# A fused attention and gated-MLP block on one core: first loads of x interleaved with the gate weights, the residual reloaded in four parts, and another hand-written order of the attention stage

## The chip, the cores and the metric

The kernel runs on one NeuronCore of a Trainium2 chip. The metric is the device time of one execution in microseconds (us). Before the change it is 266.06 us, the median of three runs (265.9 to 266.5).

## The reference

The inputs are x (2048 tokens by 512, bf16), the attention weights wqkv and wo, and the gate weights w_in, w_sp, b_sp and w_out. Cut to what matters:

```python
xn = layernorm(x)                                   # once, used by both branches
# A: attention, 32 heads of 16, a window of 256 tokens, causal
q, k, v = split(xn @ wqkv)
p = softmax(where(0 <= i - j < 256, q @ k.T / 4, -1e9))
A = (p @ v) @ wo
# B: gated MLP with mixing over tokens, F = 1376, Fh = 688
z = gelu_tanh(xn @ w_in)
z1, z2 = z[:, :Fh], layernorm(z[:, Fh:])
B = (z1 * (w_sp @ z2 + b_sp)) @ w_out
out = x + A + B
```

## The kernel before

The 2048 tokens are 16 blocks of 128. The program has no scheduler: every engine runs its instructions in the order in which the source writes them, and waits only on semaphores.

**First stage (L309 to L368).** x is loaded by SyncE (SP) in pairs of blocks (`load_x`, L189), the first pair as two single blocks. A block n goes through `stats` (L252: mean and variance on VectorE, DVE; the power -0.5 on GpSimd, POOL), `norm` (L258, DVE) and a transpose into `xnT`: blocks 0 to 5 by TensorE (PE) in `transpose_x` (L269), the others by a transposing DMA. `do_z(n, half)` (L279) multiplies block n with one half of w_in in 16 matmuls (4 chunks of the depth, columns 512 and 176), and ScalarE (ACT) applies the gelu. w_in comes in four DMAs (`load_win`, L203): two for the half z2, which `do_z(n, 1)` reads, and two for the half z1, which `do_z(n, 0)` reads. The last two, and the load of wqkv, are held back by a tiny DVE memset into the target (L313, L326). PE's order at the start is: 10 warm-up matmuls, transposes of block 0, 3 warm-up matmuls, transposes of block 1, `do_z(0, 1)`, `do_z(1, 1)`, transposes of block 2, `do_z(0, 0)`, transposes of block 3, and on.

**Attention stage (L568 to L601).** A list of tokens, `ORDER` (L49), is the order of the work. Each token issues a step:

- `qIIe`: the scores of tile II (four blocks of 128 keys by 128 queries, four head pairs), even or odd heads: PE matmuls that use a quarter of the array's rows each (L479), into two of the three double banks of the PSUM pool `ps_s`; then two exponentials on ACT (L487).
- `mII`: the masks of tile II, on POOL for a diagonal block (L498) and on DVE for the far edge of the window (L503).
- `aGw`, `AGw`: the values of head group G for a pair of query blocks w (L532, a quarter of the array's columns each), then on DVE a transpose and a reciprocal, and on POOL the division (`divide`, L546). `a` uses the single bank `ps_y`, `A` a double bank of `ps_s`; `C` and the `B` behind it share one double bank.
- `t`: DVE transposes a divided result into `oT` (L565).
- `pkGg`, `pqGg`, `pvGg` (`P`: into a bank of `ps_s`): a projection of k, q or v (L135, L151), emptied by DVE (L147, L161, L171).
- a number: so many matmuls of the token mixing w_sp @ z2 (L397). 32 of them make one block; at a block's first one, SP is given the transposing DMA of the next block of w_sp (L381). At the end of each half DVE forms z1 * (g + b) (L404), and SP transposes it for the output (`uT`, L420).
- `o`, `O`: one of the two parts of an output block: 4 matmuls with wo (L428), then 6 with w_out (L434), DVE's addition of the residual (L439), and the store (L440).

The residual: behind the last projection (L579 to L586) `xnT` is free, and SP loads x once more, into it, in four DMAs of 512 KB one after the other. The DMA for chunk c holds the blocks c, c + 4, c + 8 and c + 12.

SP's queue is in order, and holds all loads, the transposing DMAs and the stores but the last three. The matmuls of PE and their weight loads come to PE as a program of 6400 instructions, which is itself fetched by DMA while the kernel runs (queue q8 in the profile).

Of the kernel before, what the change touches and what calls it, by code (L numbers as in the profile page):

```python
# [8 lines left out]
P = 128  # L9
BF = mybir.dt.bfloat16  # L10
# [5 lines left out]
D = 512  # L16
# [5 lines left out]
NB = S_TOK // P  # L22
NDC = D // P
# [23 lines left out]


ORDER = """  # L49
pv11 Pk03 q000 1 pq03 2 q001 2 pq10 1 q010 9 m00 q011 1 pk10 q020 3 m01 2 a00 1 q021 10 q030  # L50
pk11 4 m02 q031 10 q040 2 pv03 q041 4 m03 t 1 pk12 q050 6 m04 1 q051 1 a01 3 q060 pk13 3 m05
q061 4 a02 1 q070 8 q071 a03 1 t 3 q080 pv10 2 m07 2 q081 pq11 3 m06 1 q090 pq12 4 q091 a04 3
m08 q100 2 pk20 2 q101 9 q110 pv12 1 t 1 m10 3 q111 1 pv13 1 m09 q120 5 pq21 q121 3 t 1 a05 m11
q130 2 m12 8 q131 pq20 4 q140 t t 2 pk21 q141 3 A06 a07 A10 q150 4 m13 7 q151 2 pq13 q160 m14 6
a11 q161 3 t 6 q170 1 t pv20 1 t q171 3 m16 5 m15 3 q180 4 pq23 q181 1 m17 8 q190 t a12 6 q191 1
pk23 3 m18 3 q200 6 m19 4 q201 a13 C14 B15 q210 t 2 pv21 4 q211 5 m20 3 q220 2 pk22 Pv23 3 m21
q221 3 pq31 q230 10 q231 pq30 2 m23 q240 4 pq22 2 m22 q241 7 t 1 q250 a16 1 t 3 q251 1 m24 2 t 3
Pv30 6 q260 pk32 3 t q261 2 A20 a17 A21 q270 11 q271 m26 pk30 4 q280 t 10 q281 2 pv31 4 q290 1
m25 2 m28 7 q291 2 pv22 q300 1 m27 9 q301 m29 6 A22 m30 a23 q310 8 q311 3 t 5 pk33 q320 1 m31
Pq33 3 a24 q321 2 t 7 t q330 3 pq32 t Pk31 q331 pv33 4 q340 2 m32 3 m33 3 q341 4 pv32 m34 1 q350  # L60
2 t 10 q351 3 a30 A25 t A26 a27 q360 10 q361 3 t o 1 q370 1 m35 1 o m36 q371 3 m37 5 t q380 3 o
1 q381 4 o q390 A31 a32 1 t 2 t 1 t q391 8 m39 q400 3 o 1 q401 o 1 O q410 2 O 1 o 3 m38 q411 1 o
q420 1 m40 5 A33 a34 q421 O t 2 O 1 q430 2 t m42 m41 o 1 q431 2 o q440 m43 4 O 2 O 1 A35 a36
q441 3 O m44 O o o t 5 A37 1 t O O t 2 o o 1 O O 6 O 1 O O O O O
"""


# [1 line left out]
def kernel(  # L69
# [12 lines left out]
    nc = tc.nc  # L82
    x2 = A_x.flatten_outer_dims()
# [5 lines left out]
    xnT = pers.tile([P, NDC, S_TOK], BF, name="xnT")  # L89
# [27 lines left out]
    def rpow(dst, var, n):  # L117
        v = sml.tile([P, NB], F32, name="rs_v")
        nc.vector.tensor_scalar(out=v[:, :n], in0=var, scalar1=LN_EPS, scalar2=None, op0=ALU.add)  # L119
        nc.gpsimd.tensor_tensor(out=dst, in0=v[:, :n], in1=negh[:, :n], op=ALU.pow)  # L120
# [3 lines left out]
    def bank(name, ring):  # L124
        if ring:
            return ps_s.tile([P, 2, 512], F32, name=name, tag="S")[:, 0, :]
        return ps_y.tile([P, 512], F32, name=name, tag="y")[:]
# [50 lines left out]
    with tc.tile_pool(name="win_pool", bufs=1) as winp, tc.tile_pool(  # L178
        name="xsp", bufs=8
# [6 lines left out]
        make_identity(nc, ident[:])  # L186
        xs_tiles = {}

        def load_x(n2, split=False):  # L189
            xs = xsp.tile([P, 2, D], BF, name="xs")  # L190
            if split:
                for j in range(2):
                    r = (2 * n2 + j) * P
                    nc.sync.dma_start(out=xs[:, j, :], in_=x2[r : r + P, :])  # L194
            else:
                nc.sync.dma_start(
                    out=xs[:],
                    in_=x2[2 * n2 * P : (2 * n2 + 2) * P, :].rearrange("(j p) d -> p j d", p=P),
                )
            for j in range(2):  # L200
                xs_tiles[2 * n2 + j] = xs[:, j, :]

        def load_win(half, c0, c1):  # L203
            nc.sync.dma_start(  # L204
                out=w_in_sb[:, c0:c1, half * FH : (half + 1) * FH],
                in_=B_w_in[c0 * P : c1 * P, half * FH : (half + 1) * FH].rearrange(
                    "(c p) f -> p c f", p=P
                ),
            )

        load_x(0, split=True)
        load_win(1, 0, 2)
        load_win(1, 2, 4)
        load_x(1)
        warm = sml.tile([P, 1], F32, name="warm")
        nc.scalar.activation(out=warm[:], in_=esel[:, 0:1], func=ACT.Gelu_apprx_tanh)

        nc.gpsimd.affine_select(
            out=fmask[:], in_=fmask[:], pattern=[[-1, P]], compare_op=ALU.is_gt,
# [3 lines left out]
            out=esel[:], in_=esel[:], pattern=[[-32, 4]], compare_op=ALU.is_ge,  # L223
# [3 lines left out]
            out=esel[:], in_=esel[:], pattern=[[32, 4]], compare_op=ALU.is_ge,  # L227
# [24 lines left out]
        def stats(n):  # L252
            st = sml.tile([P, nc.vector.BN_STATS_DIM], F32, name="st")
            nc.vector.bn_stats(out=st[:], in_=xs_tiles[n])  # L254
            nc.vector.bn_aggr(out=mvx[:, n, :], in_=st[:])
            rpow(rstdx[:, n : n + 1], mvx[:, n, 1:2], 1)

        def norm(n):  # L258
            xn = xnp.tile([P, D], BF, name="xn")
            nc.vector.tensor_scalar(  # L260
                out=xn[:], in0=xs_tiles[n], scalar1=mvx[:, n, 0:1],
                scalar2=rstdx[:, n : n + 1], op0=ALU.subtract, op1=ALU.mult,
            )
            if n >= X_DMA:
                nc.sync.dma_start_transpose(out=xnT[:, :, n * P : (n + 1) * P], in_=xn[:])
            else:
                xn_tiles[n] = xn
# [11 lines left out]
        def do_z(n, half):  # L279
            zp2 = ps_s.tile([P, 2, 512], F32, name="zs", tag="S")  # L280
            zp = zp2[:].rearrange("p a q -> p (a q)")
            f0 = half * FH
            for c in range(NDC):
                for lo, hi in Z_RANGES:
                    nc.tensor.matmul(  # L285
                        zp[:, lo:hi],
                        lhsT=xnT[:, c, n * P : (n + 1) * P],
                        rhs=w_in_sb[:, c, f0 + lo : f0 + hi],
                        start=(c == 0),
                        stop=(c == NDC - 1),  # L290
                    )
            dst = z1_all if half == 0 else z2_all
            nc.scalar.activation(out=dst[:, n, 0:FH], in_=zp[:, 0:FH], func=ACT.Gelu_apprx_tanh)  # L293
# [28 lines left out]
        transpose_x(1)  # L322
        do_z(0, 1)
        stats(2)
        stats(3)
        nc.vector.memset(wqkv[0:1, 0, 0:1], 0.0)  # L326
        load_x(3)
        nc.sync.dma_start(out=wqkv[:], in_=A_wqkv.rearrange("(c p) f -> p c f", p=P))
        for n2 in range(4, NB // 2):
            load_x(n2)  # L330
        norm(2)
        do_z(1, 1)
        transpose_x(2)
        stats(4)
# [3 lines left out]
            out=emask[:, 0:1], in_=esel[:], op=ALU.add, axis=mybir.AxisListType.X  # L338
        )
        nc.vector.tensor_scalar(  # L340
            out=emask[:, 1:2], in0=emask[:, 0:1], scalar1=-1.0, scalar2=1.0,
# [74 lines left out]
    def load_uT():  # L416
        n = len(uT_tiles)
        if n < NB and n < NB - (len(g_steps) + 2 * NB - 1) // (2 * NB) and n <= max(out_n[0], 0) + 3 - (out_n[0] < 0):
            uT = utp.tile([P, NFC, P], BF, name="uT")
            nc.sync.dma_start_transpose(out=uT[:], in_=z1_all[:, n, :])  # L420
            uT_tiles[n] = uT
            load_uT()

    def out_part(n, fo, c0, c1, part):
# [16 lines left out]
            out=out2[n * P : (n + 1) * P, c0:c1], in_=xr  # L441
        )

    def output(ring):
        n, part = o_steps.pop(0)
        last = n == NB - 1
        if part == 0:
            out_n[0] = n
            load_uT()
            fo_tiles[n] = bank("fo", ring)  # L450
        out_part(n, fo_tiles[n], 0, D - LAST * last, part)
        if last and part == 1:
            fo = bank("fo", not ring)
            for part in range(2):
                out_part(n, fo, D - LAST, D, part)
# [106 lines left out]
    def finish():  # L562
# [9 lines left out]
        out=w_out_sb[:, 0:5, :], in_=B_w_out[0:640, :].rearrange("(c p) n -> p c n", p=P)  # L572
# [1 line left out]
    nc.sync.dma_start(out=w_out_sb[0 : FH - 5 * P, 5, :], in_=B_w_out[5 * P : FH, :])  # L574
    tokens = ORDER.split()
    last_proj = max(i for i, t in enumerate(tokens) if t[0] in "pP")
    xres = {}
    for i, t in enumerate(tokens):
        if i == last_proj + 1:  # L579
            for n in range(NB):  # L580
                xres[n] = xnT[:, n % NDC, (n // NDC) * D : (n // NDC + 1) * D]
            for c in range(NDC):
                nc.sync.dma_start(
                    out=xnT[:, c, :].rearrange("p (m d) -> p m d", d=D),
                    in_=x2.rearrange("(m c p) d -> c p m d", p=P, c=NDC)[c],
                )  # L586
        if t[0] == "q":
            scores(int(t[1:3]), int(t[3]))
        elif t[0] == "m":
            masks(int(t[1:3]))  # L590
        elif t[0] in "aABC":
            values(int(t[1]), int(t[2]), t[0])
        elif t[0] == "t":
            finish()
        elif t[0] in "pP":
            proj(t[1], int(t[2]), int(t[3]), ring=t[0] == "P")
        elif t[0] in "oO":
            output(t[0] == "O")
        else:
            for _ in range(int(t)):  # L600
                mix()  # L601
# [30 lines left out]
```

## Time and profile before

| what | value |
|---|---|
| median of 3 runs | 266.06 us |
| the profiled execution: its time | 267.51 us |
| the profiled execution: its span, first to last instruction | 265.8 us |
| PE busy | 256.3 us, 96% |
| ACT, DVE, POOL busy | 205.6, 197.7, 122.0 us |
| granted clock of PE | 1.000 |
| mixing matmuls (L397) | 512, busy 95.1 us |
| exponentials (L487) | 180, busy 168.9 us |
| x again, as the residual | 4 DMAs of 512 KB, 5.6 us each to landing |

The page of the profile gives one execution: busy time by engine, the span in slices, the DMA queues, the chain of work that ended last, and the costliest groups of instructions. Matmuls overlap one another, so a busy PE is not one at its peak. The profiled execution took 1.45 us longer than the median, and 1.71 us of its time lie outside the span.

### The profile page before, as it was taken

The numbers are of one execution on the slowest core, as the hardware profiler recorded it, in microseconds if no ns is written. First come the engines' busy times: TensorE is split into PE (matmuls) and PEld (weight loads), VectorE is DVE, ScalarE is ACT, GpSimd is POOL, SyncE is SP. The second block draws the span as 40 slices with busy tenths as digits, with TensorE's granted clock in tenths as the row PEclk, the third lists the DMA queues.
The fourth block names the chain that finished last, engine by engine and source line by source line (L and its number), as shares of the span: only waits on it lengthen the run. The fifth ranks groups of instructions, "written<-read, shape, count | busy, mean of one in ns | idle before, by whom it ended". The sixth has DMA issues, their size and how long they took to land.

```text
span 265.8 us, 7432 instructions
## 1 busy us (share of the span) xinstructions
PE 256.3 (96%) x3166; PEld 143.1 (54%) x3199; DVE 197.7 (74%) x384; ACT 205.6 (77%) x233; POOL 122.0 (46%) x140
## 2 busy tenths in 40 slices
PE   7799999999999999999999999999998999999995
PEld 3465665654545555555575456655574454545543
DVE  4799999667687788788797778897868473686532
ACT  3577767689999999999988989988887986782000
POOL 4243445215442663758454556455468344365100
PEclk9999999999999999999999999999999999999999
DMA  6693122950405072230330323651369263434433
GB/s 212 217 337 62 39 42 59 169 180 2 109 2 112 0 111 22 62 81 2 79 81 2 79 44 41 72 52 40 81 194 226 60 131 77 73 82 71 118 78 83
DMA packets 61216, 23.83 MB, mean 90 GB/s; under 512 B 52304, under 2 KB 60672, under 8 KB 61184
## 3 DMA queue, kind: packets, MB, share of 16 engines
q1 hardware_dynamic: 60704, 23.06, 40.2%
q8 instruction: 25, 0.41, 0.7%
q10 hardware_dynamic: 432, 0.30, 0.4%
q0 software_dynamic: 48, 0.00, 0.3%
q14 instruction: 7, 0.06, 0.1%
HBM read 8.41 MB, written 2.10 MB: 40 GB/s over the span
## 4 chain that ended last, share of the span: by engine, by line
PE 93%; DMA 2%; DVE 1%; issue 1%; SPq 1%; DVEq 0%
PE gf L397 31%; PE zs L285 13%; PE S L479 12%; PE m L151 10%; PE o_t L532 8%; PE fo L434 8%; PE m L135 6%; PE fo L428 5%; DMA xs<-in_A_x_dram 2%; DVE st L254 0%; PE tp L274 0%; SPq L204 0%; DVE xnT L439 0%; SPq L194 0%; DVE o_c L548 0%
## 5 line engine op out<-in xcount | busy, mean ns | idle before, releaser
L487 ACT ACTIVATE E<-S 128x1024 bf16<-128x1024 f32 x180 | 168.9, 1043 | 17.9 <-PE S L479 9.1
L397 PE MATMUL gf<-z_all,wspT 128*128 128x344 bf16 x512 | 95.1, 311 | 1.0 <-issue 1.0
L498 POOL TENSOR_SCALAR_AFFINE_SELECT E<-E 128x1024 bf16<-128x1024 bf16 x64 | 79.2, 1259 | 32.4 <-ACT E L487 32.2
L397 PEld LDWEIGHTS <-wspT 128*128 128x128 bf16 x512 | 44.1, 98 | 36.9 <-issue 16.5
L503 DVE TENSOR_TENSOR E<-E,fmask 128x1024 bf16<-128x1024 bf16 x56 | 52.6, 967 | 2.6 <-ACT E L487 2.5
L554 POOL TENSOR_TENSOR o_norm<-o_c,rsum 128x256 bf16<-128x256 f32 x32 | 21.5, 671 | 62.0 <-DVE rsum L552 59.3
L285 PE MATMUL zs<-w_in_sb,xnT 128*128 128x512 bf16 (+1 forms) x249 | 39.1, 307 | 0.4
L479 PE MATMUL S<-q_ring,k 32*128 32x128 bf16 (+2 forms) x760 | 37.2, 267 | 0.0
L293 ACT ACTIVATE z_all<-zs 128x688 bf16<-128x688 f32 x32 | 23.8, 744 | 12.8 <-PE zs L285 12.8
L151 PE MATMUL m<-xnT,wqkv 128*128 128x512 bf16 x111 | 31.5, 380 | 1.0 <-issue 0.2
L285 PEld LDWEIGHTS <-xnT 128*128 128x128 bf16 x256 | 22.2, 98 | 14.9
L404 DVE SCALAR_TENSOR_TENSOR z_all<-gf,b_all,z_all 128x344 bf16<-128x344 f32 x32 | 18.2, 567 | 15.3 <-PE gf L397 15.3
L548 DVE STREAM_TRANSPOSE o_c<-o_t 128x512 f32<-128x512 f32 x32 | 22.3, 697 | 7.2 <-PE o_t L532 6.5
L479 PEld LDWEIGHTS <-k 32*128 32x128 bf16 x760 | 12.7, 92 | 25.9 <-issue 25.2
L439 DVE TENSOR_TENSOR xnT<-fo,xnT 128x512 bf16<-128x512 f32 (+2 forms) x17 | 11.2, 659 | 17.2 <-PE fo L434 17.2
L532 PE MATMUL o_t<-E,v 128*32 128x128 bf16 (+1 forms) x1080 | 23.4, 238 | 0.0
L434 PE MATMUL fo<-w_out_sb,uT 128*128 128x512 bf16 (+2 forms) x101 | 23.3, 366 | 0.1
L532 PEld LDWEIGHTS <-v 128*32 128x32 bf16 x1080 | 19.2, 97 | 5.1 <-issue 4.6
L120 POOL TENSOR_TENSOR rstdx<-rs_v,negh 128x1 f32<-128x1 f32 x16 | 10.3, 646 | 18.3 <-DVE rs_v L119 16.9
L171 DVE TENSOR_TENSOR k<-m,emask 128x1024 bf16<-128x1024 f32 x13 | 15.8, 1218 | 3.2 <-PE m L151 3.0
L151 PEld LDWEIGHTS <-wqkv 128*128 128x128 bf16 x128 | 11.7, 98 | 11.6 <-issue 1.7
L135 PE MATMUL m<-wqkv,xnT 128*128 128x128 bf16 x256 | 16.9, 219 | 0.2 <-DVE o_c L548 0.2
(51 smaller groups left out, 173.2 us busy)
## 6 DMA issues: line engine op xcount, KB each, us to landing
xnT<-in_A_x_dram SPq DMA_DIRECT2D x4, 512.0 KB, 5.6
xs<-in_A_x_dram SPq DMA_DIRECT2D x7, 256.0 KB, 6.7
out_dram<-xnT SPq DMA_DIRECT2D x13, 128.0 KB, 1.7
wqkv<-in_A_wqkv_dram SPq DMA_DIRECT2D x1, 1536.0 KB, 6.3
w_in_sb<-in_B_w_in_dram SPq DMA_DIRECT2D x4, 344.0 KB, 4.8
w_out_sb<-in_B_w_out_dram SPq DMA_DIRECT2D x1, 640.0 KB, 6.2
wo_sb<-in_A_wo_dram SPq DMA_DIRECT2D x1, 512.0 KB, 5.1
xs<-in_A_x_dram SPq DMA_DIRECT2D x2, 128.0 KB, 2.0
```

Of the source, the lines that this page charges most:

```text
L135: nc.tensor.matmul(m[:, j * P : (j + 1) * P], lhsT=xnT[:, c, n * P : (n + 1) * P], rhs=wqkv[:, c, 2 * D + G * P : 2 * D + (G + 1) * P], st ...
L151: nc.tensor.matmul(m, lhsT=wqkv[:, c, w0 : w0 + P], rhs=xnT[:, c, grp * 512 : (grp + 1) * 512], start=(c == 0), stop=(c == NDC - 1),)
L285: nc.tensor.matmul(zp[:, lo:hi], lhsT=xnT[:, c, n * P : (n + 1) * P], rhs=w_in_sb[:, c, f0 + lo : f0 + hi], start=(c == 0), stop=(c == NDC ...
L293: nc.scalar.activation(out=dst[:, n, 0:FH], in_=zp[:, 0:FH], func=ACT.Gelu_apprx_tanh)
L397: nc.tensor.matmul(gf[:, 0:FQ], lhsT=wsp_tiles[n][:, c, :], rhs=z2_all[:, c, lo : lo + FQ], start=(c == 0), stop=(c == NB - 1),)
L434: nc.tensor.matmul(fo[:, c0:c1], lhsT=uT_tiles[n][:, c, :], rhs=w_out_sb[:, c, c0:c1], start=False, stop=(c == NFC - 1),)
L479: nc.tensor.matmul(S[:, h2, j * P : (j + w) * P], lhsT=k_t[(G, kb // 4)][32 * s : 32 * s + 32, e, (kb % 4) * P : (kb % 4 + 1) * P], rhs=q_ ...
L487: nc.scalar.activation(out=E[:, j : j + 3 : 2, 0:nb, :].rearrange("p h b c -> p h (b c)"), in_=tiles[pr][:, :, 0 : nb * P], func=ACT.Exp, ...
L498: nc.gpsimd.affine_select(out=E[:, :, j, :], in_=E[:, :, j, :], pattern=[[0, 8], [1, P]], compare_op=ALU.is_ge, fill=0.0, base=0, channel_ ...
L503: nc.vector.tensor_tensor(out=E[:, :, j, :], in0=E[:, :, j, :], in1=fmask[:].unsqueeze(1).to_broadcast([P, 8, P]), op=ALU.mult,)
L532: nc.tensor.matmul(T[32 * s : 32 * s + 32, e, j * P : (j + l) * P], lhsT=v_t[(G, kb // 4)][:, kb % 4, s, e : e + 2, :].rearrange("p a d -> ...
L548: nc.vector.transpose(out=C[:, 0 : 32 * DH], in_=Tb)
```

## The change

There are three edits.

1. *The first loads.* `load_x` loses its split form. A new `load_block` loads one block. The order on SP was block 0, block 1, two DMAs for the z2 half of w_in, the pair of blocks 2 and 3; it is now block 0, block 1, first z2 DMA, block 2, second z2 DMA, block 3. And on DVE `norm(2)` now stands right behind `stats(2)`; it stood behind `stats(3)` and behind the memset that releases wqkv.
2. *The residual.* A new `load_xres(c)` loads the blocks 4c to 4c + 3 into chunk c of `xnT`. Part 0 is loaded behind the last projection; the parts 1, 2 and 3 when the output of the blocks 0, 4 and 8 begins, so each is asked for four blocks ahead.
3. *`ORDER`* is another list. It has the same steps: 90 score tokens, 45 mask tokens, 39 projections, 32 values, 32 `t`, 32 output parts and 512 mixing matmuls. It has 146 runs of mixing matmuls where there were 155, and two `C`/`B` pairs where there was one.

```diff
-        def load_x(n2, split=False):
+        def load_block(n):
+            if n % 2 == 0:
+                xs_pairs[n // 2] = xsp.tile([P, 2, D], BF, name="xs")
+            xs_tiles[n] = xs_pairs[n // 2][:, n % 2, :]
+            nc.sync.dma_start(out=xs_tiles[n], in_=x2[n * P : (n + 1) * P, :])
+
+        def load_x(n2):
             xs = xsp.tile([P, 2, D], BF, name="xs")
...
-        load_x(0, split=True)
+        load_block(0)
+        load_block(1)
         load_win(1, 0, 2)
+        load_block(2)
         load_win(1, 2, 4)
-        load_x(1)
+        load_block(3)
...
         stats(2)
+        norm(2)
         stats(3)
         nc.vector.memset(wqkv[0:1, 0, 0:1], 0.0)
...
-        norm(2)
         do_z(1, 1)
...
+    def load_xres(c):
+        part = xnT[:, c, :].rearrange("p (m d) -> p m d", d=D)
+        for m in range(4):
+            xres[4 * c + m] = part[:, m, :]
+        nc.sync.dma_start(
+            out=part, in_=x2[4 * c * P : (4 * c + 4) * P, :].rearrange("(m p) d -> p m d", p=P)
+        )
...
         if part == 0:
             out_n[0] = n
+            if n % 4 == 0 and n + 4 < NB:
+                load_xres(n // 4 + 1)
             load_uT()
...
         if i == last_proj + 1:
-            for n in range(NB):
-                xres[n] = xnT[:, n % NDC, (n // NDC) * D : (n // NDC + 1) * D]
-            for c in range(NDC):
-                nc.sync.dma_start(
-                    out=xnT[:, c, :].rearrange("p (m d) -> p m d", d=D),
-                    in_=x2.rearrange("(m c p) d -> c p m d", p=P, c=NDC)[c],
-                )
+            load_xres(0)
```

Of the order, two places that the prediction speaks of (before above, after below):

```diff
-a01 3 q060 pk13 3 m05 q061 4 a02
+a01 3 q060 1 m05 1 pk13 2 q061 9 q070 a02
...
-m33 3 q341 4 pv32 m34 1 q350 2 t 10 q351 3 a30 A25 t A26 a27 q360 10 q361 3 t o
+m32 pv32 1 q340 5 t 4 q341 pv30 4 m33 3 q350 m34 9 A30 A25 a26 q351 5 t 1 t 2 q360 8 o
```

More of the change, by code (lines that the diff above doesn't have):

```diff
@@ L49 @@
 ORDER = """
[L50 to L61, printed above, removed]
@@ L62 @@
-1 q381 4 o q390 A31 a32 1 t 2 t 1 t q391 8 m39 q400 3 o 1 q401 o 1 O q410 2 O 1 o 3 m38 q411 1 o
-q420 1 m40 5 A33 a34 q421 O t 2 O 1 q430 2 t m42 m41 o 1 q431 2 o q440 m43 4 O 2 O 1 A35 a36
-q441 3 O m44 O o o t 5 A37 1 t O O t 2 o o 1 O O 6 O 1 O O O O O
+Pq10 Pk03 q000 pq03 3 q001 3 pv11 q010 5 m00 5 q011 pk10 1 m01 1 q020 10 q021 4 pk11 m02 q030 8
+q031 2 a00 5 q040 1 pv03 2 q041 t 2 m03 1 pk12 q050 10 m04 q051 1 a01 3 q060 1 m05 1 pk13 2 q061
+9 q070 a02 4 q071 a03 2 t 2 q080 t pv10 m06 4 q081 pq12 4 q090 m07 pq20 2 A04 q091 pq11 1 m08
@@ new lines @@
+q100 4 pk20 q101 9 q110 pv12 2 m10 2 q111 pv13 4 q120 m09 pq21 3 q121 1 m11 4 a05 q130 t 1 m12 3
+t a06 q131 9 q140 2 t 1 Pq22 a10 A07 q141 m13 1 pk21 1 t 1 q150 9 q151 4 pq13 q160 3 t m14 6
+q161 a11 4 q170 3 pv20 1 m16 q171 2 t m15 1 pq23 1 q180 7 t 2 q181 2 pv21 m17 1 q190 m18 15 q191
+C12 B13 a14 m19 q200 9 q201 3 pv23 1 q210 3 pk23 q211 10 t q220 6 pk22 q221 1 m20 9 q230 6 pq31
+q231 2 t m21 2 a15 q240 1 t 5 m22 4 q241 2 pq30 m23 2 q250 2 t 7 q251 5 a20 C16 B17 q260 11 q261
+1 m24 pv31 4 m26 q270 pk32 4 q271 6 t 4 q280 2 pk31 q281 3 m25 1 t 2 Pk33 5 q290 5 t a21 q291 2
@@ new lines @@
+m27 7 q300 a22 2 m28 5 q301 Pq32 pv22 Pk30 q310 11 q311 4 m29 1 a23 A24 q320 pq33 1 t 3 q321 9
+m31 1 q330 1 m30 1 pv33 t q331 6 m32 pv32 1 q340 5 t 4 q341 pv30 4 m33 3 q350 m34 9 A30 A25 a26
+q351 5 t 1 t 2 q360 8 o m35 q361 t 2 t 4 m36 2 q370 3 o 1 q371 4 m37 o q380 o 3 q381 A31 a32 A27
+t q390 8 q391 2 m38 3 o q400 o q401 1 m39 7 t O 1 t q410 2 O m40 o 3 q411 2 o 2 q420 A33 a34 4 t
+t 2 q421 m42 1 o 1 q430 1 o O 1 q431 O 1 o m41 q440 1 m43 o O 2 O A35 a36 t t q441 O O 2 O O o
+m44 o 2 A37 O 3 t 5 O 4 o o O O O O
@@ L187 @@
         xs_tiles = {}
-        def load_x(n2, split=False):
-            xs = xsp.tile([P, 2, D], BF, name="xs")
[L191 to L195, printed above, removed]
-                nc.sync.dma_start(
-                    out=xs[:],
-                    in_=x2[2 * n2 * P : (2 * n2 + 2) * P, :].rearrange("(j p) d -> p j d", p=P),
-                )
+        xs_pairs = {}
+        def load_block(n):
[4 more added lines that the diff above has]
+        def load_x(n2):
+            xs = xsp.tile([P, 2, D], BF, name="xs")
+            nc.sync.dma_start(
+                out=xs[:],
+                in_=x2[2 * n2 * P : (2 * n2 + 2) * P, :].rearrange("(j p) d -> p j d", p=P),
+            )
             for j in range(2):
@@ L442, in out_part @@
         )
+    xres = {}
+    def load_xres(c):
+        part = xnT[:, c, :].rearrange("p (m d) -> p m d", d=D)
+        for m in range(4):
+            xres[4 * c + m] = part[:, m, :]
+        nc.sync.dma_start(
+            out=part, in_=x2[4 * c * P : (4 * c + 4) * P, :].rearrange("(m p) d -> p m d", p=P)
+        )
     def output(ring):
@@ L576 @@
     last_proj = max(i for i, t in enumerate(tokens) if t[0] in "pP")
-    xres = {}
     for i, t in enumerate(tokens):
         if i == last_proj + 1:
-            for n in range(NB):
-                xres[n] = xnT[:, n % NDC, (n // NDC) * D : (n // NDC + 1) * D]
-            for c in range(NDC):
-                nc.sync.dma_start(
-                    out=xnT[:, c, :].rearrange("p (m d) -> p m d", d=D),
-                    in_=x2.rearrange("(m c p) d -> c p m d", p=P, c=NDC)[c],
-                )
+            load_xres(0)
         if t[0] == "q":
```

## The prediction

> **What bounds the kernel now.** I read the page first: the busy times, then the shares of the chain that ended last.
>
> ```profile
> PE 256.3 (96%) x3166; PEld 143.1 (54%) x3199; DVE 197.7 (74%) x384; ACT 205.6 (77%) x233; POOL 122.0 (46%) x140
> ...
> PE 93%; DMA 2%; DVE 1%; issue 1%; SPq 1%; DVEq 0%
> ```
>
> PE is the bound, in both stages. So only two things can move the time: holes in PE's work, and PE work that becomes longer or shorter. ACT, DVE and POOL matter where they make PE wait. Next I went through PE's rows in order of time and looked for steps longer than the same step elsewhere. There are two large holes. The first is near the start. In the chain in order of time:
>
> ```profile
> 2.71 5.55 DMA xs<-in_A_x_dram
> 8.28 0.70 DVE st L254
> 9.38 0.61 DVE st L254
> 10.39 0.35 DVE xn L260
> 10.78 0.40 PE tp L274 x4
> 11.18 1.17 PE zs L285 x8
> ```
>
> Blocks 2 and 3 land at 8.26. DVE then makes the statistics of both before it norms block 2. PE had finished `do_z(1, 1)`, and its transposes of block 2 begin at 10.78. The timeline gives the hole ahead of them:
>
> ```profile
> 10.78 0.40 PE L274 MATMUL tp<-ident,xn 128*128 128x128 bf16 x4 [1.79 <-DVE xn L260]
> ```
>
> The second hole is at 202, two score tokens after the residual loads. From PE's and SP's timelines there:
>
> ```profile
> 201.63 0.41 PE L479 MATMUL S<-q_ring,k 32*128 32x384 bf16 x8
> 203.02 0.61 PE L397 MATMUL gf<-z_all,wspT 128*128 128x344 bf16 x3 [0.98 <-issue]
> ...
> 194.08 2.03 SPq L583 DMA_DIRECT2D xnT<-in_A_x_dram  x4
> 197.40 6.16 SPq L381 DMA_TRANSPOSE wspT<-in_B_w_sp_dram  x1
> ```
>
> The same pair of steps takes 0.34 elsewhere and 1.39 here: 1.05 us lost, in which PE waited for nothing that the profile shows. The DMA rows of two windows, 188 to 200.5 and 200.5 to 206, give the reason that I take:
>
> ```profile
> q14 instruction: 1, 0.01, 0.2%
> ...
> q8 instruction: 2, 0.03, 2.4%
> ```
>
> q8 moves PE's program, 25 transfers in all (page). 0.41 MB for a program of 6400 instructions is one transfer per 256. In the 12.5 us before 200.5 there is none, though PE issued some 480 instructions in them; then come two in 5.5 us. Meanwhile the four residual loads keep the DMA engines full (204 GB/s and a DMA share of 0.95 over 194 to 208). I read the hole as PE out of instructions, because the fetch came late. Besides these two, the attention stage loses some 0.9 us in pieces of at most 0.3.
>
> **First loads.** Blocks 0 and 1, and the first z2 DMA, keep their places; that DMA lands at 5.0 (1.73 issue, 3.3 to landing). The next 344 KB landed 0.98 us later (2.19 + 3.8), so 128 KB cost about 0.36: block 2 lands near 5.4, the second z2 DMA near 6.35 instead of 6.0. `do_z(0, 1)` starts at 6.50 and needs that DMA for its fifth to eighth pair of matmuls, from about 7.1: covered by 0.7. DVE is free at 6.2. Block 2 takes 0.69 statistics, 0.18, 0.15, POOL's 0.55, 0.41 norm, with gaps 2.2 in all (the rows from 8.28 on), so it is normed at 8.4, and PE, done near 8.9, finds it ready. `norm(2)` now waits some 0.7 for POOL with `stats(3)` behind it on DVE; block 3 isn't there before 8.26, so this costs nothing as long as it lands then. SP has one more issue (0.45) ahead of the loads of the z1 half; those waited for DVE's memset until 4.04 anyway.
>
> The hole closes, but what is late next? `do_z(0, 0)` would start at 9.1 and needs the z1 half. Its two DMAs have the same bytes ahead of them as before, and the slowest load of w_in took 6.4 from its issue at 4.45: 10.84. Then half of that step is left, 1.17/2 = 0.58, so block 3's transposes come at 11.48 instead of 12.18: **-0.7**, not -1.9. Block 3 is normed by then (8.45 plus two statistics and a norm: 10.96). From there to 56 us PE has no hole in the trace and everything hangs on PE's own pace, so the 0.7 is carried. Bounds: 15 of the 16 parts of each of these loads landed about 1.5 us earlier than the last, so one DMA engine was late. Without it in a run, block 3's norm sets the transposes: 12.18 - 11.04 = -1.1 against this trace. But a run without it had little hole before either: blocks 2 and 3 at 6.7, transposes of block 3 at 10.75, and DVE's wait for POOL now makes that 11.04: **+0.3**. I take -0.7, the value of the rows.
>
> **Residual in four parts.** Part 0 alone stands ahead of the next w_sp transpose, 512 KB instead of 2 MB. A transposing DMA's issue took 6.16 behind four loads and 1.45 to 1.95 without; behind one I estimate 3. PE's fetch waits behind a quarter as much. The parts 1 to 3 go into SP's queue ahead of a uT transpose and a store; the uT is used three blocks later, and each part four blocks later, over 10 us against 5.6 to landing. Part 0 is asked for some 8 us of PE work before the first output part: covered; without that cover DVE's addition, and with it the bank, would wait. So the hole goes: **-1.05**. Bounds: 0 (the loads are not its cause) and -1.05.
>
> The Trainium skill, page "DMA: Bandwidth & Descriptors", section "Queues, rings and completion order", speaks against this: each DMA engine takes turns between its queues, a packet at a time. By that rule a fetch on its own queue would not stand behind 2 MB of another, the hole would stay, and the sum would be -1.0. The trace leans the other way (no q8 transfer for 12.5 us, then two in 5.5).
>
> **The order.** The same matmuls are issued, so I count the joints. A mixing run takes 0.143 a matmul. Followed by a projection, its last one takes 0.16; followed by scores or values, 0.25. So each step from the whole array into its row or column parts costs 0.1. There are 93 in the old list, 91 in the new: -0.2. Nine fewer runs of mixing and the other neighbours (medians of each token by what follows it) make up to -0.46. I take **-0.3**.
>
> New waits? The bank `ps_y` first. From the end of one user to the start of the next, less DVE's row for emptying it (v and q 0.69, k 1.22, values 0.69 to 0.72), the old list has 0.04 too little once (`pk10` to `a00`), and 0.19 once; the smallest in the new is 0.33 (outputs aside). Values: `A30` comes 4.1 after `q341`, where `a30` came 5.1 after. The mask takes 0.44 + 2 x 0.92 for the exponentials and 1.09 to 1.55 on POOL: 3.4 to 3.9. Just enough; bound +0.3. The two `C`/`B` pairs hold a double bank for some 3 us; behind each stand 9 or 11 mixing matmuls before the second score token: 0. ACT needs 1.81 per score token and gets one every 1.8 to 2.0 in the first 60 us in both lists: 0. The tail ends with four output parts and the same last store: 0.
>
> Sum: -0.70 - 1.05 - 0.30 = -2.05. The profiled 267.51 would become 265.5; the median, 1.45 lower, 266.06 - 2.05 = **264.0**.
>
> **The rivals.**
>
> - *The start gives nothing* (the late DMA engine belongs to the profiled run): for it, the 1.45 that this run lies above the median is just the engine's lateness. 266.06 + 0.3 - 1.35 = 265.0; at +0 264.7.
> - *The second hole stays*: the loads did not hold the fetch up, and PE stops there for a reason of its own place in the program. The trace shows no request, so this is open; 266.06 - 1.0 = 265.05. It is what the rule of the Trainium skill's page above would make of it.
> - *Masks hold up DVE.* In `m05 1 pk13` the mask now stands ahead of k's emptying, and `a02` needs the bank. DVE's masks took 0.627 to 1.585 (median 0.692, mean 0.967), long where POOL masks run beside them. With all at 1.57, three places hold PE (`m02` 0.35, `m05` 0.97, `m26` 0.37): +1.7, 265.7. The old list has one, 0.6.
> - *All goes well*: the hole at the start closes fully and the small waits halve: 266.06 - 1.8 - 1.05 - 0.7 = 262.5.
> - *Slower: each part starves PE once.* Four separate bursts, each ahead of a transposing DMA, instead of one. If every one costs what the block of four cost, 4 x 1.05 in place of 1.05 is +3.15, less 1.0: 268.2. From three on (+2.1 - 1.0) it is slower, 267.2. Against it: a w_sp transpose moves 512 KB too (128 x 2048 bf16), and twelve of them passed in the attention stage ahead of the residual loads without such a hole.
>
> **How the numbers follow.** A change of 0.2%, 0.53 us, is about what a measurement of this kernel can tell. Chances: forecast 0.38 (264.0); start nothing 0.20; hole stays 0.11; masks 0.08 (half of it within 0.2%); all well 0.08; both first rivals together, 266.0, 0.03; slower 0.12. Faster: 0.38 + 0.20 + 0.11 + 0.04 + 0.08 = 0.81; same 0.04 + 0.03 = 0.07; slower 0.12. The range leaves out the slower case and some of the best: 262.6 to 266.6. The forecast's own range is 263.3 to 264.6.
>
> **What the new profile would show.** Block 2's transposes right behind `do_z(1, 1)`, near 8.9; a shorter hole inside `do_z(0, 0)` that ends when the last w_in DMA lands; block 3's transposes near 11.5. No hole over 0.5 in PE behind the first residual part, and q8 transfers without a gap of 12 us. PE's steps from the first to the last token sum to 0.2 to 0.5 less. I am wrong if PE's rows have new holes in front of values tokens (masks), or in "issue" behind each residual part.

## The result

The changed kernel takes 265.97 us (median, 265.56 to 266.07), and the kernel before, run beside it, 266.43 (265.9 to 267.74). The ratio is 0.9978, with a 95% interval of 0.997 to 0.9986. So it is faster, as forecast, but by some 0.5 us where 2.05 were forecast. The time lies inside the range given. It is also where the rival "both first rivals together" (266.0) had it, but that is chance: that rival keeps the second hole, and the hole went.

The two profiled executions differ by more: 267.51 and 266.03 us, spans 265.8 and 264.3. Here and below, rows of a view that do not matter are left out between those shown. The page of the changed kernel, its busy times and the first shares of its chain:

```profile
span 264.3 us, 7431 instructions
...
PE 256.7 (97%) x3168; PEld 143.2 (54%) x3199; DVE 198.6 (75%) x384; ACT 206.0 (78%) x233; POOL 121.0 (46%) x140
...
PE 70%; DVE 13%; ACT 8%; issue 3%; DMA 3%; POOL 1%; SPq 0%; POOLq 0%; DVEq 0%
```

PE is as busy as before, but its share of the chain fell from 93% to 70%, and DVE and ACT came in with 13% and 8%. The chain now leaves PE at one wait, 55.91 us into the span, and follows DVE, POOL and ACT back from there through the first stage. So the shares tell where the chain runs, and not how much was lost. Two places answer to what the prediction showed, and two holes are new.

The start, from the chain of the changed kernel in order of time:

```profile
4.68 5.85 DMA w_in_sb<-in_B_w_in_dram
10.57 0.74 PE zs L290 x4
11.32 0.22 PE tp L279 x4
```

The second z1 load lands at 10.53, the second half of `do_z(0, 0)` follows at once, and block 3's transposes begin at 11.15 by PE's own rows (the chain counts them from 11.32, when the matmuls ahead of them have ended), 1.03 us earlier than the 12.18 in the trace of before. That is the mechanism of the forecast, and a little more than its 0.7.

The place of the second hole, from PE's timeline and from the DMA rows of the window 188 to 200.5:

```profile
199.81 0.41 PE L496 MATMUL S<-q_ring,k 32*128 32x384 bf16 x8
200.15 1.34 PE L402 MATMUL gf<-z_all,wspT 128*128 128x344 bf16 x8
201.33 1.03 PE L433 MATMUL fo<-wo_sb,oT 128*128 128x512 bf16 x3
...
q8 instruction: 1, 0.02, 0.8%
```

The hole is gone, and a program fetch now stands in the window that had none: by the packets of the two traces it comes at 197.52, where it came at 200.58.

And two holes that were not there. The first is in the first score token (timeline, 52.5 to 60):

```profile
54.35 0.83 DVE L309 TENSOR_SCALAR z_all<-z_all,mv,rstd 128x688 bf16<-128x688 bf16 x2 [0.81 <-POOL rstd L120]
55.17 0.68 DVE L161 CAST q_ring<-m 128x512 bf16<-128x512 f32 x1
55.34 0.39 PE L496 MATMUL S<-q_ring,k 32*128 32x384 bf16 x4
55.91 0.40 PE L496 MATMUL S<-q_ring,k 32*128 32x384 bf16 x4 [0.17 <-DVE q_ring L161]
```

The token breaks in the middle: its second half waits for DVE to empty a double bank, and DVE comes to that only after it has normed the last blocks of z2. `Pq10 Pk03 q000` asks for four double banks, and there are three. This costs 0.55 us. The second is at `a02` (timeline, 75 to 83):

```profile
78.33 1.03 PE L151 MATMUL m<-xnT,wqkv 128*128 128x512 bf16 x3
78.40 2.63 DVE L520 TENSOR_TENSOR E<-E,fmask 128x1024 bf16<-128x1024 bf16 x2
78.94 1.55 POOL L515 TENSOR_SCALAR_AFFINE_SELECT E<-E 128x1024 bf16<-128x1024 bf16 x1
80.96 1.21 DVE L171 TENSOR_TENSOR k<-m,emask 128x1024 bf16<-128x1024 f32 x1
82.22 0.84 PE L549 MATMUL o_t<-E,v 128*32 128x128 bf16 x32 [0.48 <-DVE k L171]
```

The two masks of `m05` take 2.63 us beside a mask on POOL, and stand ahead of k's emptying, which frees the bank for the values. 0.55 us again.

From the first projection in `ORDER` to the start of the last output step PE's rows take 205.87 us where they took 206.43 in the trace of before. What of this is waiting I can only estimate: the sum of the steps without any wait, each at its median of before, falls by some 0.46 (204.49 to 204.02), and what PE loses besides goes from 1.94 to 1.85. So the hole of 1.05 went, and 0.96 of other waits came. The rest of the 1.5 us between the spans is the start.

### The profile page after: what moved, and what is told of

Its sections match the earlier page's. It is cut to its first block, busy times and chain, and to the rows that moved or that the text cites. A ratio compares the mean times of both kernels' runs of the same rounds, so it can differ in the third digit from the quotient of the medians.

```text
span 264.3 us, 7431 instructions
## 1 busy us (share of the span) xinstructions
PE 256.7 (97%) x3168; PEld 143.2 (54%) x3199; DVE 198.6 (75%) x384; ACT 206.0 (78%) x233; POOL 121.0 (46%) x140
## 4 chain that ended last, share of the span: by engine, by line
PE 70%; DVE 13%; ACT 8%; issue 3%; DMA 3%; POOL 1%; SPq 0%; POOLq 0%; DVEq 0%
PE gf L402 26%; PE S L496 10%; PE o_t L549 8%; PE fo L439 8%; ACT E L504 8%; PE m L151 7%; PE fo L433 5%; PE m L135 4%; PE zs L290 3%; DVE st L303 3%; DMA w_in_sb<-in_B_w_in_dram 2%; DVE z_all L309 2%; DVE st L259 2%; DVE E L520 2%; DVE xn L265 1%
## 5 line engine op out<-in xcount | busy, mean ns | idle before, releaser
L402 PE MATMUL gf<-z_all,wspT 128*128 128x344 bf16 x512 | 93.2, 310 | 0.0
L515 POOL TENSOR_SCALAR_AFFINE_SELECT E<-E 128x1024 bf16<-128x1024 bf16 x64 | 78.0, 1241 | 29.1 <-ACT E L504 28.9
L520 DVE TENSOR_TENSOR E<-E,fmask 128x1024 bf16<-128x1024 bf16 x56 | 53.6, 979 | 2.8 <-ACT E L504 2.6
```

The source lines that it names most:

```text
L402: nc.tensor.matmul(gf[:, 0:FQ], lhsT=wsp_tiles[n][:, c, :], rhs=z2_all[:, c, lo : lo + FQ], start=(c == 0), stop=(c == NB - 1),)
L515: nc.gpsimd.affine_select(out=E[:, :, j, :], in_=E[:, :, j, :], pattern=[[0, 8], [1, P]], compare_op=ALU.is_ge, fill=0.0, base=0, channel_ ...
L520: nc.vector.tensor_tensor(out=E[:, :, j, :], in0=E[:, :, j, :], in1=fmask[:].unsqueeze(1).to_broadcast([P, 8, P]), op=ALU.mult,)
```

## The experiments

Each kernel was timed in turn with the kernel before. "PE's stretch" is the time of PE's rows from the first projection in `ORDER` to the start of the last output step, in the one profiled execution of each kernel; "block 3" is the start of block 3's transposes.

| kernel | median us | ratio to before (95%) | block 3 | PE's stretch |
|---|---|---|---|---|
| before, the trace of the prediction | 266.43 | 1 | 12.18 | 206.43 |
| after | 265.97 | 0.9978 (0.997 to 0.9986) | 11.15 | 205.87 |
| e1 before again | 266.50 | 1.0005 (0.9996 to 1.0013) | 10.65 | 206.68 |
| e2 first edit alone | 266.46 | 1.0008 (1.0 to 1.0017) | 10.93 | 206.35 |
| e3 residual in parts alone | 265.29 | 0.9961 (0.9949 to 0.9974) | 10.97 | 205.39 |
| e4 new order alone | 265.85 | 0.9982 (0.9973 to 0.999) | 11.51 | 205.99 |
| e5 all but the order | 265.50 | 0.9963 (0.9951 to 0.9975) | 10.77 | 205.41 |
| e6 after, two tokens moved | 264.76 | 0.9934 (0.9921 to 0.9946) | 10.90 | 205.02 |
| e7 first loads alone | 266.41 | 1.0002 (0.9993 to 1.0011) | 10.59 | 206.48 |
| e8 residual loaded twice | 266.68 | 1.0008 (0.9996 to 1.002) | 10.96 | 206.35 |
| e9 burst behind the w_sp transpose | 265.51 | 0.9966 (0.9952 to 0.9979) | 10.99 | 205.38 |
| e10 e6 and a third token | 264.99 | 0.9945 (0.9932 to 0.9957) | 10.76 | 205.17 |

### e1: the kernel before, a second trace

> The kernel before, unchanged, for a second trace. Its first profiled execution took 267.51 us, 1.1 above the median of 19 runs (266.43). Theory 1: the extra 1.1 is the late DMA engine at the start (blocks 2 and 3 at 8.26 instead of 6.7, the hole of 1.8 ahead of block 2's transposes); then another execution near the median has a hole of at most 0.8 there, and still has the hole of 1.05 behind the residual loads near 202. Theory 2: the extra is the hole near 202, which is then missing here, while the hole at the start stays at about 1.8. Ratio 1.000 in both.

The chain of this trace at the start:

```profile
2.71 4.03 DMA xs<-in_A_x_dram
6.76 0.71 DVE st L254
7.86 0.61 DVE st L254
8.86 0.35 DVE xn L260
9.25 0.40 PE tp L274 x4
```

Blocks 2 and 3 land at 6.73, not 8.26. Block 2's transposes come at 9.25 and the hole ahead of them is 0.27, not 1.79. The hole near 200 is there, and larger:

```profile
200.13 0.41 PE L479 MATMUL S<-q_ring,k 32*128 32x384 bf16 x8
201.75 0.61 PE L397 MATMUL gf<-z_all,wspT 128*128 128x344 bf16 x3 [1.21 <-issue]
```

So the first theory holds. This execution took 266.22 us, 1.29 less than the first profiled one, and block 3's transposes stand 1.53 earlier. The start that the prediction was built on was that of an execution well above the median.

### e2 and e7: the first edit, whole and without the moved norm

e2 is the kernel before with the first edit alone. e7 leaves `norm(2)` where it was (against e2):

```diff
         stats(2)
-        norm(2)
         stats(3)
...
         for n2 in range(4, NB // 2):
             load_x(n2)
+        norm(2)
```

> Only the first edit (order of the first loads, block 2 normed ahead of block 3's statistics); residual and order of the attention stage as before. Theory 1: the hole at the start is mostly the late engine of one execution, so the edit is worth 0 to 0.3 us: ratio 0.999 to 1.000. Theory 2: the edit is worth the 1.03 us by which block 3's transposes came earlier in the traces: ratio 0.996.

> The kernel before with the first loads interleaved, but block 2 normed at its old place, behind block 3's statistics. In an execution without a late DMA engine the hole ahead of block 2's transposes was 0.4 us, and in the kernel with the whole first edit DVE's wait for POOL brought block 3's transposes 0.28 later. So: the loads alone gain 0.2 to 0.4 (block 3's transposes near 10.4), ratio 0.999; the rival, that the second z2 DMA landing 0.36 later costs what block 2's earlier landing gains, gives 1.000.

Ratios 1.0008 and 1.0002: no gain. Over the five traces with the old start other than the first (e1, e3, e4, e8, e9) block 3's transposes lie at 10.65 to 11.51, and over the traces with the new one at 10.59 to 11.15. The late part of a load differs as much. Of the loads issued at the start, from 1.7 to 5.3 us, the last of the 16 parts landed up to 1.5 us behind the other fifteen in before, 0.7 in e4, 0.4 to 0.7 in after, e5, e6 and e7, and not over 0.25 in the others. What the edit does lies inside this scatter. The 0.2 to 0.4 that I expected of the loads alone did not show in the time.

### e3, e4 and e5: the residual and the order, alone and together

e3 is the kernel before with `load_xres`, e4 the kernel before with the new `ORDER` alone, e5 the changed kernel with the old `ORDER`.

> Only the second edit (the residual in four parts). Theory 1: the hole of 1.05 us near 202 is in every run and goes: ratio 0.996. Theory 2: the hole was in the one profiled execution alone, or has nothing to do with the loads: ratio 0.999 to 1.000.

> Only the third edit (the other ORDER), with the four residual loads still in one burst. By the two traces the order's joints are worth -0.46 us, and its new waits (0.55 at the first score token, 0.55 at a02, some 0.1 at three more places, less those of the old list) cost about +0.95: slower by 0.5, ratio 1.002. If the new waits were of that one execution alone, faster by 0.4, ratio 0.9985. A hole behind the burst of loads should still be seen, of about 1 us, if the burst makes it.

> The changed kernel with the old ORDER. My theory: the hole behind the residual loads is one thing, and either the parts or the new order takes it away; so with the parts in place the new order has only its joints (-0.46) and its waits (+0.95) left, and costs 0.5. Then this kernel is faster than the changed one by about 0.5 us: 265.4, ratio to before 0.996. Rival: the gains of the single edits add up (0.9961 for the residual, 0.9982 for the order), something else in the changed kernel lost 0.9, and this one stands no better than 0.996 only if the first edit costs nothing; if the first edit disturbs the later stages, 0.998.

The parts alone are worth 1.0 us, the whole of the hole. In e3's trace PE's rows at that place run on (timeline, 198.5 to 203):

```profile
200.43 0.41 PE L491 MATMUL S<-q_ring,k 32*128 32x384 bf16 x8
200.77 0.61 PE L397 MATMUL gf<-z_all,wspT 128*128 128x344 bf16 x3
```

In e4's trace both new waits stand as in the changed kernel (0.55 at the first score token, 0.55 at `a02`), yet e4 is faster than before by 0.5. PE's timeline behind the burst shows why:

```profile
200.29 0.41 PE L479 MATMUL S<-q_ring,k 32*128 32x384 bf16 x8
200.63 1.34 PE L397 MATMUL gf<-z_all,wspT 128*128 128x344 bf16 x8
201.80 1.03 PE L428 MATMUL fo<-wo_sb,oT 128*128 128x512 bf16 x3
```

There is no hole, though the four loads are in one burst. The fetch was late here too, but the new order had issued fewer instructions by then.

Count two instructions for each weight load, in fetches of 256, from the beginning of the fetch before this one. PE was at 1.48 when this fetch started in e4 (at 201.0), at 1.64 to 1.67 in the five traces with the hole (before, e1, e2, e7, e8), and at 0.81 and 0.91 in e3 and e5. In those five PE stops at the same instruction, 1.77 on this count, and goes on 1.3 to 1.6 us after the packet of the fetch has ended. In e4, e3 and e5 it comes to that count 3.1 to 3.5 us after it, and does not stop. That fits an engine that has run out of instructions; it does not fit a stop that belongs to the place in the program, since e3 and e5 pass the same instruction. What passes in the 1.3 to 1.6 us the profile does not show. My expectation of e4 had the hole stay; it was wrong there.

So the parts and the order take away the same hole, and it can be saved only once. With the parts in both, the order costs: e5 to after, 205.41 to 205.87 of PE's stretch, +0.46. With the joints estimated at -0.46, that leaves some +0.93 of waits. In the medians it is 265.50 against 265.97.

### e6 and e10: the new waits taken out

Against the changed kernel, e6 has:

```diff
-Pq10 Pk03 q000 pq03 3 q001 3 pv11
+pq10 Pk03 q000 3 pq03 q001 3 pv11
...
-q060 1 m05 1 pk13 2 q061
+q060 2 pk13 m05 2 q061
```

e10 has these, and `2 q080 t 3 pv10 m06 1 q081` in place of `2 q080 t pv10 m06 4 q081`.

> The changed kernel, with its two new waits taken out of the order: the first q projection of group 1 goes into the single bank and three mixing matmuls ahead of the next one, and the masks m05 stand behind pk13. If the two waits of 0.55 are real losses, about -1.0 against the changed kernel: 265.0, ratio to before 0.9945. If PE only waits elsewhere for the same thing (DVE is late all along there), less than -0.3: ratio 0.997.

> The kernel with the two tokens moved, and pv10 three mixing matmuls later, to take out the wait of 0.3 us for the single bank that both orders have in front of it. If it goes without a new one: -0.3 against the kernel with two tokens moved (264.76), 264.5, ratio 0.9923. If the wait moves on to the next step, no difference: 0.9934.

e6 is 1.2 us faster than the changed kernel, and the fastest version here (0.9934). DVE now empties k first, and the values token follows without a wait:

```profile
78.66 1.22 DVE L171 TENSOR_TENSOR k<-m,emask 128x1024 bf16<-128x1024 f32 x1 [1.13 <-PE m L151]
79.80 1.28 DVE L520 TENSOR_TENSOR E<-E,fmask 128x1024 bf16<-128x1024 bf16 x2
80.94 0.84 PE L549 MATMUL o_t<-E,v 128*32 128x128 bf16 x32
```

The masks themselves take 1.28 for two here instead of 2.63; the POOL mask has ended by then (at 79.30). PE's share of the chain is back at 93%. PE's stretch fell by 0.85 (205.87 to 205.02), and not by the 1.10 of the two waits. Most of the rest is a new stop of 0.2: a score token at 131.38 takes 0.63 where it takes 0.43 in the changed kernel, and PE goes on 1.4 us after the packet of a program fetch, as at the hole near 200. That it is the same thing is likely and not tested. In e10 the third wait only moved:

```profile
85.97 0.41 PE L496 MATMUL S<-q_ring,k 32*128 32x128 bf16 x8
86.68 1.02 PE L151 MATMUL m<-xnT,wqkv 128*128 128x512 bf16 x4 [0.30 <-DVE v L147]
```

PE now waits 0.36 one token later, for DVE to empty what `pv10` left. e10 is no faster than e6. Two values tokens and two projections follow each other through one bank there, and by these rows DVE's work between them does not fit.

### e8 and e9: what the fetch waits for

Both are against the kernel before, e8 first:

```diff
-            for c in range(NDC):
+            for c in [0, 1, 2, 3, 0, 1, 2, 3]:
```

```diff
-        if i == last_proj + 1:
+        if i == last_proj + 16:
```

> The kernel before, with the four residual loads issued twice, one burst of 4 MB (the second time into the same place, so that each waits for the first of its kind). If PE's program is fetched late because of the burst, the fetch that came at 199.2 comes some 5 to 6 us later and the hole of 1.28 us grows to 5 to 7: ratio 1.02. If each DMA engine takes turns between its queues (the rule of the Trainium skill's page on DMA), the fetch comes at the same time and the hole stays near 1.3: ratio 1.000 to 1.003. A wait of the mixing matmuls for the w_sp transpose behind the burst would show as a DMA releaser, from about 212 on.

> The kernel before with the four residual loads still in one burst of 2 MB, but one place later in SP's queue, behind the w_sp transpose, so that they start near 198 instead of 192.6. Theory: a program fetch waits for the loads that are already queued when it is asked for (near 196), not for later ones; then the fetch comes at about 196.4 as with the residual in parts, the hole is gone, and the ratio is 0.996. Rival: a burst of 2 MB in this stretch starves PE wherever it stands; then a hole of about 1 us appears some 3 to 5 us later, ratio 1.000.

In e8 the hole did not grow (PE's timeline, and the DMA rows of 198 to 200.5):

```profile
200.44 0.41 PE L479 MATMUL S<-q_ring,k 32*128 32x384 bf16 x8
201.74 0.61 PE L397 MATMUL gf<-z_all,wspT 128*128 128x344 bf16 x3 [0.89 <-issue]
...
q8 instruction: 1, 0.02, 2.8%
```

The fetch comes at 199.01, in e1 at 199.18. My 5 to 7 us were wrong, and hole and ratio are what I had put down for engines that take turns. But e8 doesn't decide it: the second four loads were issued only from 196.79 on, as each waited for the first of its kind, so they were hardly queued when the fetch was due. The theory of e9 is that a fetch waits for loads that are queued when it is asked for, and not for later ones. In e9 the burst starts at 198.57 (SP's timeline), and the window 195 to 197 shows the fetch alone, at 196.99:

```profile
DMA packets 1, 0.02 MB, mean 8 GB/s; under 512 B 0, under 2 KB 0, under 8 KB 0
...
q8 instruction: 1, 0.02, 3.0%
```

The hole is gone, and 0.9966 is as good as the parts. So it is not the 2 MB, nor the stretch of the program, but four loads queued ahead of just this fetch. The next fetch of e9 shows the same from the other side: it falls into the burst and is late (202.91; 201.54 and 200.34 in e3 and e5), but PE comes to 1.77 on its count only 7.4 us after that packet, and nothing is lost.

How much of the queue the fetch waits for is less than the theory says. In the six traces with the burst (before, e1, e2, e4, e7, e8) it starts while the parts of the third load land, or at most 0.33 us before the first of them. In e8 the first parts of the four loads land at 196.20, 197.70, 199.22 and 200.64, and the fetch starts at 199.01. The fourth load had been issued by 194.92, and one of its parts lands 0.9 us behind the other fifteen, which fits a fetch of 1.1 us that went ahead of it. So the fetch does not seem to wait for everything that was queued before it. No record shows when it is asked for; that it was near 196 is taken from the traces with one load or none in its way.

## Why the prediction was right and wrong

- **The residual: -1.05, right.** e3 gives -1.04 by its ratio (0.0039 x 266.45), and PE's stretch in it is 0.96 to 1.29 shorter than in the five traces with the hole. Its cause, a late fetch of PE's program when the loads are queued ahead of it, is borne out by e9 and by the place at which PE stops. The sign that I read it from is weaker than it looked. A gap of 12.5 us between fetches says little by itself; the changed kernel has one of 13.4 (230.28 to 243.66) without a hole. What counts is how many instructions PE has issued. The rule of the Trainium skill, page "DMA: Bandwidth & Descriptors", section "Queues, rings and completion order", that an engine takes turns between its queues by packets, would have kept the hole. Here the hole went with the burst, and with the old order the fetch comes at 196.4 to 197.0 with one load or none ahead (e3, e5, e9) and at 199.0 to 199.2 with four (e1, e2, e7, e8). But by the landings it gets ahead of the fourth load. What it waits for, and whether turns are taken further on, no run shows.
- **The start: -0.70, wrong; the step that failed is "I take -0.7, the value of the rows".** The late z1 half does set block 3 where parts of it land late: the trace of after even shows -1.03. But the row was that of one execution with a late DMA engine, and the medians are not. Without one, as in e2, PE waits 0.31 for DVE, which has normed block 3 just before (transposes at 10.93); the prediction had this as its bound of +0.3 (11.04). e2 gives +0.2 (ratio 1.0 to 1.0017), e7 none: the term measures 0 to +0.2, for -0.70. The page of the profile had said so: the profiled time stood 1.45 above the median, and the late part of the loads was about 1.5. I worked this out as the first rival and gave it 0.20, and kept the larger value because it came from a row. (10.84 and 0.58 also make 11.42 and not 11.48, a slip of 0.06.)
- **The order: -0.30, wrong by its sign; the step is "New waits?".** Against -0.30, e5 to after measures +0.46. The joints can't be told apart from small waits; that e6, without the two new waits, has 0.39 less of PE's stretch than e5 is near the -0.46 of the medians. The waits did not come out at 0. Two things failed. For the single bank I compared PE's gaps with the row of the emptying alone, as if DVE were free; at `a02` it was behind two masks. The third rival had just this place and priced it at 0.97; it measured 0.55. Its other two places cost nothing. And I checked the double banks for the `C`/`B` pairs, but not for the first token, where `Pq10 Pk03 q000` needs a fourth; that one cost 0.55 too. These two make 1.10, and less the waits that the old list had of its own the balance is the +0.93.
- **The sum.** The start at 0, -1.05 for the hole, -0.46 and +0.93 for the order make -0.6. Measured are -0.59 by the ratio (0.0022 x 266.43) and -0.46 by the two medians. The direction, and the range, came from the residual.
- **The slower rival**, that each part starves PE once, did not occur: the changed kernel's trace has no hole marked by issue behind any part.

## What to carry to other kernels

Before a hole in a trace is given a price, compare the profiled time with the median: if the execution is slower by about the size of the hole, the hole may be that execution's alone, and a second trace of the same kernel settles it. When an order written by hand is changed, check each bank against what stands ahead of its emptying in the emptying engine's queue, not against the emptying alone; and count the banks that the first tokens ask for. A burst of loads can stop an engine that uses none of the data, by holding up the fetch of its program when the engine is near the end of what was fetched: split the burst, or move it behind the fetch.

## What was not expected of the hardware

PE waited here for something that is no semaphore. Its program comes in 25 fetches for 6400 instructions, and a fetch that started 2.0 to 2.8 us late (199.0 to 199.2 against 196.4 to 197.0) left PE idle for 0.88 to 1.21 us, with nothing in the profile to wait for. The same lateness cost nothing where PE had issued fewer instructions meanwhile (e4). Of the loads issued in the first 12 us, one of the 16 parts landed 1.0 to 1.6 us behind the other fifteen in eight of the twelve traces: in before on five loads issued at 2.7 to 5.0 us, in the other seven on a load issued at about 11 us; why is open. And two masks on DVE took 2.63 us beside a mask on POOL (the changed kernel), 1.28 us with none (e6).
